# A fused attention and feed-forward kernel on one core: wider stores of the last block, a merged projection burst, a new sequence

## The chip, the cores and the metric

The kernel runs on one core of one Trainium2 chip. The metric is the device time of one execution in microseconds (us), as the median of several runs. The engines are TensorE (PE; its weight loads are PEld), VectorE (DVE), ScalarE (ACT), GpSimd (POOL) and SyncE (SP), which computes nothing and only issues DMAs. ACT and POOL issue DMAs too.

## The reference

Eight batches of eight heads go through linear attention with 128 random features; the result, 4608 rows of 512, goes through a two-layer feed-forward network with a hard-swish.

```python
def phi(x):                              # x: q or k, scaled; omega: (128, 64)
    proj = np.einsum('bhsd,md->bhsm', x, omega)
    h = proj - np.sum(x * x, axis=-1, keepdims=True) / 2.0
    return np.exp(h - np.max(h, axis=-1, keepdims=True)) / np.sqrt(m)
kv = np.einsum('bhsm,bhsd->bhmd', k_p, v); z = np.sum(k_p, axis=2)
num = np.einsum('bhsm,bhmd->bhsd', q_p, kv)
attn = num / (np.einsum('bhsm,bhm->bhs', q_p, z)[..., None] + 1e-06)
x = attn.transpose(0, 2, 1, 3).reshape(4608, 512)
h = x @ w_in                             # (512, 2048)
out = (h * np.clip(h + 3.0, 0.0, 6.0) / 6.0) @ w_out   # (2048, 512), float32
```

## The kernel before

**Tiling.** A batch has 576 rows: 512 "main" rows and 64 leftover rows. Attention runs batch by batch (`attention(b)`, b from 0 to 7). The feed-forward part runs over nine blocks of 512 rows: block b is the main rows of batch b, and block 8 is the 64 leftover rows of all eight batches, gathered in the tile `xS`. So partition p of block 8's output is row 512 + (p mod 64) of an even batch (p below 64) or of the odd batch after it (p from 64), and the four groups of 128 rows, r = 0 to 3, are the four pairs of batches. In the output tensor the two halves of a group lie 576 x 512 elements apart.

**Projections.** For b of 3 and more the products of k and q with omega are issued in bursts (`burst`, lines 749 to 798; matmuls at lines 766 and 769). A burst covers a few column groups ("doubles" of 128 rows) of k and q. A burst of two doubles takes two PSUM banks, one of four doubles takes four; the ring has eight banks in all. `BURSTS` gives five bursts per batch: one of two doubles (the leftover rows) and four of four doubles (main rows). ACT reads each bank with an exponential (kp at line 785, qpT at line 794), and DVE takes a row maximum.

**Feed-forward.** The first layer is `mm1` (line 1047); in blocks 7 and 8 it is a seven-product form of a 2 x 2 block product (`mm1_pair`, line 1126). The second layer is `products(blk)` (line 1305), called P0 to P6 here, again a seven-product form. DVE adds the pieces (line 1321): u3 after P3, C22 after P4, u4, and C21 after P5; ACT copies C11 (line 522). For block 8 the seventh product is cut into three pieces by `last_product` (matmuls at line 1371, additions C12 at line 1379): piece 0 is 256 columns wide, pieces 1 and 2 are 128 wide. Sums of activations that these products need are called S1 to S4 (line 1233), on POOL, some of block 8's on DVE.

**Stores of block 8.** `store` (DMA at line 1400) writes the three quarters C22, C21 and C11, each as two DMAs of 64 partitions by two row groups by 256 columns (128 KB). `last_product` (DMA at line 1383) writes each of its three pieces as two DMAs of 64 partitions (64 KB, and 32 KB for the narrow pieces). So there are twelve DMAs, on SP or ACT. Their destination patterns start with 64 rows, for instance `x[a, MAIN:S, 2 * i:2 * i + 2, c0:c1]` with the half `a` fixed: rows, then row groups, then columns. Blocks 0 to 7 are written by DMAs of 128 partitions from SP.

**What sets the order.** Every operation gets a number in the order in which the code creates it. `ORDER` lists, by these numbers, which operations each engine runs and in which sequence; an operation that two engines may run stands in the list of the one that does. Waits follow from the data. A list is strictly in order: what stands behind a waiting operation waits too. With the costs in the code the planner only orders the merged program; the numbers in `ORDER` fix the sequence on each engine. At the end the program waits for all stores.

Of the kernel before, what the change touches and what calls it, by code (L numbers as in the profile page):

```python
# [20 lines left out]
        118, 13, 124, 139, 144, 156, 115, 150, 168, 147, 153, 133, 127, 121, 142, 162, 165, 183, 171, 159, 175, 177,  # L21
        136, 185, 212, 130, 173, 197, 214, 179, 219, 254, 199, 187, 181, 242, 227, 189, 204, 202, 257, 229, 244, 217,
        222, 403, 404, 232, 234, 415, 247, 416, 417, 409, 410, 249, 411, 405, 406, 412, 418, 207, 421, 424, 252, 237,
        260, 280, 427, 430, 433, 300, 436, 288, 284, 282, 439, 286, 442, 306, 303, 445, 290, 315, 324, 309, 448, 451,
        312, 292, 294, 454, 296, 318, 457, 298, 333, 321, 583, 584, 331, 573, 337, 574, 335, 575, 339, 585, 586, 587,
        327, 341, 588, 576, 353, 345, 589, 343, 577, 329, 355, 366, 578, 579, 593, 368, 379, 371, 594, 595, 358, 392,
        590, 384, 381, 394, 397, 580, 374, 596, 597, 598, 361, 387, 603, 400, 599, 600, 621, 627, 624, 639, 636, 604,
        630, 642, 645, 505, 651, 492, 660, 501, 654, 495, 657, 486, 605, 507, 511, 606, 503, 607, 474, 509, 666, 483,
        498, 477, 480, 672, 608, 669, 513, 489, 609, 792, 610, 675, 519, 782, 515, 517, 527, 783, 539, 798, 541, 544,
        532, 551, 785, 529, 786, 563, 793, 556, 565, 568, 553, 695, 795, 796, 702, 799, 801, 802, 723, 805, 806, 709,  # L30
        736, 809, 815, 716, 824, 812, 818, 830, 741, 827, 839, 833, 842, 748, 854, 848, 845, 750, 860, 738, 760, 857,
        772, 753, 863, 765, 970, 774, 777, 971, 762, 980, 973, 974, 981, 883, 986, 983, 984, 890, 987, 989, 990, 897,
        1003, 1000, 1012, 997, 993, 994, 1006, 911, 1015, 924, 1021, 1027, 929, 1018, 936, 1033, 1030, 904, 926, 1048,
        1042, 1036, 941, 938, 1045, 960, 1051, 1174, 1158, 1159, 965, 948, 962, 1168, 953, 950, 1161, 1071, 1169,
        1162, 1078, 1171, 1172, 1175, 1085, 1177, 1178, 1191, 1092, 1185, 1188, 1194, 1200, 1215, 1203, 1112, 1206,
        1209, 1218, 1181, 1182, 1124, 1117, 1224, 1221, 1230, 1236, 1114, 1099, 1239, 1233, 1126, 1136, 1346, 1347,
        1129, 1141, 1138, 1356, 1148, 1349, 1150, 1153, 1350, 1357, 1259, 1287, 1359, 1360, 1266, 1362, 1365, 1366,
        1273, 1363, 1379, 1376, 1373, 1382, 1388, 1300, 1394, 1369, 1302, 1312, 1391, 1305, 1314, 1397, 1370, 1317,
        1406, 1336, 1409, 1418, 1338, 1403, 1421, 1412, 1280, 1424, 1427, 1550, 1341, 1534, 1535, 1544, 1454, 1537,
        1545, 1447, 1324, 1538, 1326, 1329, 1547, 1548, 1461, 1551, 1553, 1468, 1557, 1554, 1488, 1475, 1490, 1558,  # L40
        1500, 1493, 1561, 1502, 1505, 1512, 1579, 1517, 1514, 1567, 1582, 1524, 1570, 1526, 1600, 1529, 1591, 1564,
        1615, 1609, 1594, 1576, 1606, 1585, 1612, 1660, 1673, 1597, 1663, 1629, 1665, 1676, 1702, 1630, 1668, 1678,
        1689, 1632, 1633, 1692, 1639, 1694, 1705, 1681, 1718, 1707, 1640, 1697, 1731, 1721, 1642, 1723, 1643, 1734,
        1710, 1747, 1736, 1648, 1649, 1760, 1726, 1750, 1739, 1807, 1645, 1763, 1752, 1646, 1765, 1820, 1755, 1810,
        1652, 1812, 1653, 1836, 1768, 1823, 1776, 1825, 1815, 1777, 1839, 1849, 1828, 1841, 1779, 1852, 1865, 1844,
        1854, 1780, 1878, 1868, 1786, 1857, 1870, 1881, 1787, 1894, 1883, 1792, 1907, 1873, 1886, 1897, 1789, 1899,
        1793, 1790, 1910, 1902, 1939, 1912, 1795, 1796, 1915, 1799, 1800, 1923, 1924, 1933, 1934, 1926, 1927, 1936,
        1937, 1940, 1943, 1944, 1960, 1952, 1956,
    ],
    "SP": [  # L50
        0, 21, 17, 32, 23, 22, 31, 19, 25, 26, 27, 24, 29, 28, 30, 269, 270, 271, 469, 473, 472, 471, 470, 592, 602,
        468, 688, 467, 582, 693, 402, 692, 691, 694, 612, 689, 547, 535, 690, 559, 571, 572, 880, 879, 881, 804, 876,
        756, 744, 808, 768, 780, 882, 877, 781, 878, 992, 1067, 996, 1069, 1068, 1070, 932, 1065, 944, 968, 956, 969,
        1066, 1064, 1255, 1184, 1257, 1256, 1258, 1180, 1120, 1252, 1253, 1144, 1132, 1156, 1157, 1254, 1440, 1443,
        1445, 1446, 1368, 1372, 1444, 1441, 1320, 1442, 1344, 1308, 1332, 1345, 1496, 1520, 1508, 1532, 1556, 1560,
        1533, 1651, 1655, 1798, 1802, 1950, 1948, 1949, 1947, 1962, 1959,
    ],
    "ACT": [
        18, 20, 138, 119, 140, 145, 141, 157, 148, 154, 169, 151, 134, 166, 143, 211, 163, 184, 135, 172, 160, 196,
        176, 178, 241, 174, 186, 213, 225, 226, 180, 243, 182, 203, 190, 218, 188, 233, 407, 413, 419, 422, 425, 281,  # L60
        238, 261, 431, 253, 434, 428, 301, 289, 285, 437, 440, 287, 307, 443, 304, 446, 310, 449, 316, 452, 313, 455,
        325, 319, 297, 299, 295, 352, 334, 322, 336, 340, 332, 458, 342, 328, 338, 354, 378, 377, 330, 367, 344, 380,
        346, 393, 375, 362, 388, 401, 622, 591, 628, 625, 640, 631, 581, 601, 637, 643, 652, 646, 493, 661, 506, 655,
        496, 658, 502, 508, 512, 487, 504, 475, 478, 481, 673, 484, 499, 490, 667, 510, 526, 514, 611, 676, 538, 670,
        516, 520, 528, 518, 540, 550, 784, 561, 562, 787, 564, 696, 698, 700, 708, 705, 707, 703, 731, 726, 729, 701,
        724, 735, 728, 715, 714, 710, 737, 712, 816, 717, 810, 719, 813, 721, 819, 746, 828, 759, 831, 825, 840, 843,
        834, 770, 846, 722, 849, 761, 771, 855, 773, 861, 864, 858, 972, 888, 886, 884, 891, 893, 889, 896, 895, 900,
        975, 1004, 1001, 902, 898, 903, 920, 923, 998, 1013, 1007, 914, 912, 916, 1016, 1022, 1019, 1028, 917, 1034,
        1031, 907, 905, 910, 909, 1043, 1037, 946, 1049, 1052, 947, 1046, 1160, 949, 1076, 1072, 1074, 1163, 1084,
        1083, 1081, 1079, 1077, 1086, 1090, 1088, 1091, 1093, 1192, 1095, 1111, 1186, 1098, 1189, 1201, 1204, 1195,  # L70
        1134, 1123, 1207, 1216, 1210, 1125, 1097, 1225, 1219, 1222, 1231, 1237, 1102, 1100, 1105, 1137, 1234, 1240,
        1104, 1348, 1149, 1351, 1264, 1262, 1265, 1293, 1288, 1292, 1267, 1271, 1260, 1290, 1272, 1269, 1274, 1276,
        1296, 1299, 1380, 1295, 1279, 1374, 1311, 1377, 1383, 1278, 1389, 1395, 1313, 1392, 1334, 1335, 1398, 1407,
        1337, 1410, 1419, 1404, 1422, 1413, 1281, 1283, 1285, 1425, 1286, 1428, 1536, 1459, 1457, 1455, 1460, 1450,
        1448, 1539, 1453, 1452, 1484, 1464, 1462, 1467, 1466, 1487, 1469, 1471, 1473, 1489, 1499, 1476, 1478, 1501,
        1480, 1481, 1474, 1513, 1562, 1523, 1568, 1525, 1580, 1571, 1592, 1565, 1583, 1601, 1595, 1577, 1607, 1586,
        1613, 1661, 1662, 1674, 1598, 1664, 1675, 1610, 1677, 1616, 1631, 1669, 1690, 1671, 1691, 1703, 1693, 1682,
        1706, 1684, 1719, 1698, 1720, 1711, 1700, 1722, 1732, 1733, 1735, 1713, 1727, 1748, 1749, 1740, 1762, 1729,
        1742, 1751, 1764, 1809, 1756, 1758, 1811, 1769, 1822, 1816, 1771, 1824, 1837, 1818, 1840, 1850, 1831, 1829,
        1853, 1845, 1866, 1847, 1867, 1858, 1879, 1869, 1880, 1860, 1882, 1874, 1895, 1887, 1889, 1898, 1876, 1909,  # L80
        1903, 1911, 1905, 1916, 1918, 1928, 1946, 1951, 1955, 1963, 1954, 1958,
    ],
    "DVE": [
        16, 10, 11, 5, 4, 12, 123, 15, 7, 14, 125, 8, 116, 146, 9, 126, 191, 158, 128, 122, 155, 6, 209, 170, 167,
        152, 149, 239, 194, 129, 161, 164, 224, 131, 137, 198, 220, 200, 255, 201, 215, 221, 228, 216, 256, 230, 245,
# [317 lines left out]
def _emit(nc, es, q, k, v, omega, w_in, w_out, out):  # L403
    B, H, S, D = q.shape
# [11 lines left out]
    MAIN = 512  # L416
    TU = [(0, 2), (2, 6), (6, 10), (10, 14), (14, 18)]
    HALVES = [(0, 2), (2, 4)]
    SPLIT = 3
    ROWS = 3  # L420
    BURSTS = [[(0, 2)], [(2, 6)], [(6, 10)], [(10, 14)], [(14, 18)]]
    RP = 2.0
    FAST = 4
    APACE = 0.06
# [80 lines left out]
    op = G.op  # L505
# [987 lines left out]
```

The softmax here doesn't subtract the row's maximum and nothing guards it: scores larger than these inputs give would overflow.

## Time and profile before

| what | value |
|---|---|
| median of 3 runs | 308.26 us (307.58 to 308.68) |
| the profiled execution | 308.06 us |
| its span in the trace | 306.2 us |
| granted TensorE clock, mean | 0.998 |
| PE busy | 297.7 us (97%) |
| DVE busy | 245.7 us (80%) |
| POOL busy | 233.7 us (76%) |
| ACT busy | 212.8 us (69%) |
| median DMA of 128 KB, output from SP, issue to landing | 2.5 us |
| last matmul starts / ends | 301.17 / 301.39 us |

The time of an execution is about 1.9 us longer than the span that the trace covers. A busy PE is a modelled quantity: matmuls overlap. Times below are counted from the start of the span. The DMA rows give packets, megabytes and the time that the packets took as a share of sixteen DMA engines over the window that was asked for, so that share x 16 x window is the engine time used.

### The profile page before, as it was taken

The page shows a single profiled execution, that of the slowest core. Times are in us where ns is not written, and L with a number is a line of the kernel's source. Part 1 is how long each engine was busy: PE and PEld are TensorE (multiplying, and loading weights), DVE is VectorE, ACT ScalarE, POOL GpSimd, SP SyncE. Part 2 cuts the span into 40 slices and gives each one's busy share as a digit, 9 for nine tenths or more (in the row PEclk, how much of TensorE's full clock was granted, in tenths as well). Part 3 has the DMA queues.
Part 4 walks back from the last instruction along what each step waited for, and adds up shares of the span by engine and source line. Part 5 has one row for each costly group of instructions (what it writes and reads, how often), then busy time and mean ns, then how long its engine had stood idle before and what let it go on. Part 6 is the DMA issues. An engine that isn't in the chain of part 4 may idle for free.

```text
span 306.2 us, 7368 instructions
## 1 busy us (share of the span) xinstructions
PE 297.7 (97%) x2798; PEld 210.4 (69%) x2798; DVE 245.7 (80%) x539; ACT 212.8 (69%) x511; POOL 233.7 (76%) x247
## 2 busy tenths in 40 slices
PE   7999999999999999999999999999999999999993
PEld 5668866545785468646856586647764788888883
DVE  3978887779898885798596877896889898999953
ACT  4995997578959972889477758876875876675300
POOL 2775657089894989799989896988845999999950
PEclk9999999999999999999999999999999999999999
DMA  8999999999972999999949984998906000210125
GB/s 224 297 187 187 269 163 153 209 206 181 194 187 35 165 143 182 242 155 208 175 104 124 217 222 112 131 130 215 207 20 190 9 0 3 94 45 3 69 88 120
DMA packets 90147, 44.88 MB, mean 147 GB/s; under 512 B 57984, under 2 KB 87808, under 8 KB 90112
## 3 DMA queue, kind: packets, MB, share of 16 engines
q1 hardware_dynamic: 62368, 30.98, 43.5%
q0 software_dynamic: 26592, 12.46, 34.1%
q10 hardware_dynamic: 1152, 0.98, 1.2%
q8 instruction: 22, 0.36, 0.5%
q14 instruction: 13, 0.11, 0.2%
HBM read 36.73 MB, written 9.44 MB: 151 GB/s over the span
## 4 chain that ended last, share of the span: by engine, by line
PE 79%; POOL 10%; DMA 4%; DVE 2%; issue 1%; SPq 1%; ACT 1%; POOLq 0%
PE p L1305 28%; PE p L1047 25%; PE p L1126 5%; PE p L1217 4%; POOL gT L1233 3%; PE p L1192 3%; PE p L978 3%; DMA wi<-in_moe_w_in_dram 3%; POOL s L1233 3%; PE p L950 2%; PE p L766 2%; PE p L769 2%; DMA q<-in_q_dram 1%; SPq L621 1%; PE p L830 1%
## 5 line engine op out<-in xcount | busy, mean ns | idle before, releaser
L1047 PE MATMUL p<-xT,wi 128*128 128x512 f16 x384 | 90.3, 379 | 0.0
L1055 DVE SCALAR_TENSOR_TENSOR gT<-tsb,p 128x512 f16<-128x512 f16 x96 | 62.8, 679 | 12.4 <-ACT tsb L1053 11.6
L1053 ACT ACTIVATE tsb<-p 128x512 f16<-128x512 f32 x96 | 55.4, 600 | 16.5 <-PE p L1047 12.3
L1047 PEld LDWEIGHTS p<-xT,wi 128*128 128x128 f16 x384 | 35.4, 98 | 38.0 <-issue 1.1
L1305 PE MATMUL p<-wo,gT 128*128 128x256 f16 x368 | 45.8, 273 | 0.1
L1233 POOL TENSOR_TENSOR s<-gT 128x512 f16<-128x512 f16 x30 | 34.8, 1161 | 6.8 <-DVE gT L1055 4.8
L1233 POOL TENSOR_TENSOR gT<-gT,s 128x512 f16<-128x512 f16 x31 | 35.8, 1155 | 5.2 <-PE p L1305 3.0
L1233 POOL TENSOR_TENSOR s<-gT,s 128x512 f16<-128x512 f16 x31 | 35.8, 1156 | 4.9 <-DVE gT L1055 2.9
L1305 PEld LDWEIGHTS p<-wo,gT 128*128 128x128 f16 x368 | 35.0, 98 | 6.1 <-issue 0.8
L1233 POOL TENSOR_TENSOR gT<-gT 128x512 f16<-128x512 f16 x31 | 36.1, 1164 | 2.4
L934 POOL TENSOR_TENSOR vc<-v,cc 128x512 bf16<-128x512 f32 x24 | 25.4, 1057 | 12.3 <-DVE cc L928 7.4
L790 DVE TENSOR_REDUCE mx<-kp 128x4 f32<-128x512 bf16 (+1 forms) x50 | 29.9, 619 | 5.0 <-ACT kp L785 5.0
L794 ACT ACTIVATE qpT<-p 128x512 bf16<-128x512 f32 (+1 forms) x50 | 26.9, 564 | 8.6 <-PE p L769 8.6
L785 ACT ACTIVATE kp<-p 128x512 bf16<-128x512 f32 (+1 forms) x50 | 26.2, 559 | 9.3 <-PE p L769 8.6
L1305 PE MATMUL p<-t,gT 128*128 128x256 f16 x256 | 31.4, 273 | 0.0
L994 DVE TENSOR_TENSOR xb<-p,rec 128x256 f16<-128x256 f32 (+1 forms) x64 | 28.8, 471 | 0.6
L621 POOL DMA_DIRECT2D qb<-in_q_dram x28 | 19.5, 705 | 11.5 <-PE p L1047 9.6
L1305 PEld LDWEIGHTS p<-t,gT 128*128 128x128 f16 x256 | 24.3, 98 | 5.1 <-issue 1.2
L522 ACT COPY p<-p 128x256 f32<-128x256 f32 (+1 forms) x46 | 17.7, 398 | 13.2 <-PE p L1126 5.6
L1174 ACT ACTIVATE tsb<-p 128x512 f16<-128x512 f32 x32 | 18.8, 598 | 6.5 <-PE p L1126 3.9
L621 POOL DMA_DIRECT2D kb<-in_k_dram x21 | 16.5, 786 | 7.1 <-PE p L1047 7.1
L1176 DVE SCALAR_TENSOR_TENSOR gT<-tsb,p 128x512 f16<-128x512 f16 x32 | 21.0, 679 | 0.9 <-ACT tsb L1174 0.8
(132 smaller groups left out, 580.4 us busy)
## 6 DMA issues: line engine op xcount, KB each, us to landing
v<-in_v_dram SPq DMA_DIRECT2D x14, 512.0 KB, 4.9
out_dram<-osb SPq DMA_DIRECT2D x14, 512.0 KB, 3.3
kb<-in_k_dram POOLq DMA_DIRECT2D x14, 256.0 KB, 5.4
qb<-in_q_dram POOLq DMA_DIRECT2D x14, 256.0 KB, 5.6
wo<-in_moe_w_out_dram POOLq DMA_DIRECT2D x8, 256.0 KB, 8.2
wi<-in_moe_w_in_dram POOLq DMA_DIRECT2D x3, 512.0 KB, 7.4
q<-in_q_dram SPq DMA_DIRECT2D x4, 256.0 KB, 4.5
vl<-in_v_dram SPq DMA_DIRECT2D x8, 128.0 KB, 4.1
```

Source lines behind the costliest of these rows:

```text
L621: lambda E: E.dma_start(dst, src), prio + 0.001 * turn_of[0], reads=gate, writes=keys,
L785: op("ACT", actt(128 * (d1 - d0)), lambda E, lh=lh, ko=ko, part=part: E.activation(ko, out_of(part, 0, lh)[0].rearrange("p (x m) -> p x m" ...
L790: op("DVE", dvet(128 * (d1 - d0)), lambda E, ko=ko, mo=mo: E.reduce_max(mo, ko, axis=AX.X), p0 + 0.01, reads=[("kp", 0, d, lh) for d in ra ...
L794: op("ACT", actt(128 * (d1 - d0)), lambda E, lh=lh, part=part: E.activation(qd[:, part[0]:part[1], lh, :], out_of(part, 1, lh)[0].rearrang ...
L934: return E.tensor_tensor(vcm[:, :, 0:D], v32[:, m, :, :], cbc, ALU.mult)
L994: op("DVE", dvet(128 * n), lambda E: E.tensor_tensor(xv(i0, i1), psum()[:, :, :, 0:64], rbc, ALU.mult), t + 0.01, reads=[vn, ("rec", ru)], ...
L1047: ins = E.matmul(ring.t[vh.slot], wi[:, c, 128 * f:128 * f + 128], xv[:, c, :], start=(c == 0), stop=(c == NJ - 1))
L1053: op("ACT", actt(512), lambda E: E.activation(tsb[tu][:], ring.t[vh.slot], AF.Relu, bias=0.5, scale=1.0 / 6.0), t - 0.1, reads=[vh], write ...
L1055: op("DVE", dvet(512), lambda E: E.scalar_tensor_tensor(gT[gu][:, f, :], tsb[tu][:], 1.0, ring.t[vh.slot], ALU.min, ALU.mult), t - 0.1, re ...
L1176: op("DVE", dvet(512), lambda E, v=v, tu=tu, dst=dst: E.scalar_tensor_tensor(dst(), pieces(tsb[tu][:]), 1.0, pieces(v.ring.t[v.slot]), ALU ...
L1233: op(engines, {"POOL": 0.07 + n / 455.0, "DVE": 0.1 + n / 850.0}, lambda E: E.tensor_tensor(dst, x, y, ALU.subtract if minus else ALU.add) ...
L1305: ins = E.matmul(ring.t[v.slot][:, 256 * j:256 * j + 256], a[:, f, 128 * j:128 * j + 128], w[:, f, :], start=(first and f == 0 and j == 0) ...
```

## The change

Three things change.

1. The last block's stores take 128 partitions each. Each quarter is now two DMAs, one for each row group r, of 128 partitions by 256 columns (128 KB), and each piece of the last product is one DMA. That makes nine. The destination pattern now starts with the two halves `a`, then the 64 rows, then the columns.
2. `BURSTS` merges the leftover doubles with the first four main doubles into one burst that takes six PSUM banks. There are four bursts per batch instead of five, for b = 3 to 7.
3. All five lists of `ORDER` are new. The five burst operations and three stores that are gone shift the numbers: the main sequence of operations is otherwise the same, so a number below 702 means the same operation as before, and from there on it is one to five lower (up to eight lower at the very end).

With the numbers counted out, PE's list ends P3, P3, P4, then pieces 2 and 1 of the last product, P5, P5, piece 0. It used to end P3, P3, P4, P5, P5, pieces 2, 0, 1. On SP the last block's stores are now C22 (r = 2), C11 (r = 1), C11 (r = 0), piece 1, C21 (r = 2); on ACT C22 (r = 3), piece 2, C21 (r = 3), piece 0. Before, SP began with one half of C11. On DVE, S4 number 3 of block 8 now stands before u3; it stood between u3 and C22. S4 number 2 moves from POOL to DVE, also before u3.

```diff
 ORDER = {
     "PE": [
...
-        1937, 1940, 1943, 1944, 1960, 1952, 1956,
...
+        1790, 1791, 1910, 1897, 1928, 1918, 1919, 1794, 1795, 1929, 1921, 1922, 1931, 1932, 1935, 1953, 1950, 1938,
+        1939, 1947,
     "SP": [
...
-        1533, 1651, 1655, 1798, 1802, 1950, 1948, 1949, 1947, 1962, 1959,
...
+        1555, 1650, 1646, 1793, 1797, 1941, 1946, 1945, 1952, 1943,
     "ACT": [
...
-        1903, 1911, 1905, 1916, 1918, 1928, 1946, 1951, 1955, 1963, 1954, 1958,
...
+        1942, 1955, 1944, 1949,
...
-    BURSTS = [[(0, 2)], [(2, 6)], [(6, 10)], [(10, 14)], [(14, 18)]]
+    BURSTS = [[(0, 2), (2, 6)], [(6, 10)], [(10, 14)], [(14, 18)]]
...
-            for x in range(2):
-                op(("SP", "ACT"), {"SP": 0.9 * w / 1024, "ACT": 0.9 * w / 1024}, lambda E, x=x, j=j, e0=e0, e1=e1: E.dma_start(
-                    ends[x, MAIN:S, j, 256 + e0:256 + e1], osb[64 * x:64 * x + 64, j, 256 + e0:256 + e1]),
-                   t, reads=[("osb", j, 1, n)], writes=[("out", 8, j, e0, x)], group="doutl%d_%d" % (n, x), inc=16, lat=1.1,
-                   name="outl%d" % n, issue=0.65, packet=84.0)
+            op(("SP", "ACT"), {"SP": 1.8 * w / 1024, "ACT": 1.8 * w / 1024}, lambda E, j=j, e0=e0, e1=e1: E.dma_start(
+                ends[:, MAIN:S, j, 256 + e0:256 + e1], osb[:, j, 256 + e0:256 + e1]),
+               t, reads=[("osb", j, 1, n)], writes=[("out", 8, j, e0)], group="doutl%d" % n, inc=16, lat=1.1,
+               name="outl%d" % n, issue=0.65, packet=84.0)
...
         if blk < 8:
-            parts = [(0, 128, out[blk * S:blk * S + MAIN, :].rearrange("(p r) e -> p r e", r=4)[:, 2 * i:2 * i + 2, c0:c1])]
+            parts = [(2 * i, 2, out[blk * S:blk * S + MAIN, :].rearrange("(p r) e -> p r e", r=4)[:, 2 * i:2 * i + 2, c0:c1])]
         else:
             x = out.rearrange("(t a s) e -> a s t e", a=2, s=S)
-            parts = [(64 * a, 64, x[a, MAIN:S, 2 * i:2 * i + 2, c0:c1]) for a in range(2)]
+            parts = [(r, 1, x[:, MAIN:S, r, c0:c1]) for r in (2 * i, 2 * i + 1)]
...
+            src = osb[:, r:r + n, c0:c1] if n > 1 else osb[:, r, c0:c1]
```

## The prediction

> **What bounds the kernel now.** I read the page first, then the chain of waits over the last 20 us, then the timeline of PE and the DMA view of the last block's stores.
>
> ```profile
> span 306.2 us, 7368 instructions
> ...
> PE 297.7 (97%) x2798; PEld 210.4 (69%) x2798; DVE 245.7 (80%) x539; ACT 212.8 (69%) x511; POOL 233.7 (76%) x247
> ...
> PE 79%; POOL 10%; DMA 4%; DVE 2%; issue 1%; SPq 1%; ACT 1%; POOLq 0%
> ```
>
> PE is busy for 297.7 of 306.2 us. Of the other 8.5 us, 4.8 lie behind the last matmul (306.2 - 301.4), where the last stores are issued and land. By the table of busy time by stretches, 2.04 us lie in the first 10 us, 1.05 in the next 20, and so only some 0.6 in the rest. A new sequence has little idle time to win; the tail has 4.8 us.
>
> ```profile
> 299.63 1.33 PE p L1371 x16
> ...
> 300.99 0.42 DVE osb L1379
> ...
> 301.43 0.29 DVE osb L1379
> ```
>
> This is the end of the chain: the last product (L1371), then DVE's additions. After it only DMAs run. The timeline:
>
> ```profile
> 298.20 0.68 DVE L1321 TENSOR_TENSOR osb<-p,u 128x512 f32<-128x512 f32 x1
> ...
> 301.44 2.60 ACTq L1383 DMA_DIRECT2D out_dram<-osb  x4
> 302.35 1.24 SPq L1383 DMA_DIRECT2D out_dram<-osb  x2
> ```
>
> The first row is C22. The other two show that the issues queue: six stores of the last product, about 0.65 us each, keep ACT issuing until 304.04.
>
> **Part 1, the stores: how many DMA engines work.** The DMA view from 295.5 to 305.1 us holds just the last block's twelve stores.
>
> ```profile
> DMA packets 1344, 1.05 MB, mean 109 GB/s; under 512 B 192, under 2 KB 1344, under 8 KB 1344
> ...
> q1 hardware_dynamic: 736, 0.59, 29.1%
> q10 hardware_dynamic: 608, 0.46, 21.6%
> ```
>
> 192 tiny packets for twelve stores are 16 each: I read that as one closing packet from each of 16 engines. The two shares are 50.7% of 16 engines over 9.6 us: 77.9 us of engine time for the block's 1024 KB. Spread over 16 engines that is 4.9 us, well hidden under the issues.
>
> All twelve stores have a destination that begins with 64 rows, and every other transfer here begins with 64 or 128: each divides into 16 equal shares along its first dimension. The new destinations begin with a dimension of **two** (the halves of a pair, far apart in memory), then the 64 rows. No row shows how such a transfer is shared out. The bounds are 16 engines, as in every row, and two engines, if the sharing goes along the first dimension, as all rows would allow. I take two: rows and halves can't be joined into one dimension of 128, since they are not evenly spaced, and the code names no other cut.
>
> The Trainium skill, page "DMA: Bandwidth & Descriptors", section "Why a DMA increments its semaphore by 16 and not by 1", speaks against this change: the number of engines is the largest up to 16 that divides the slowest dimension of both sides. By it the new stores run on two engines, 64 packets of 1 KB each, where the old ones ran on 16; no row here shows a transfer below 16. The same page's section "Rules for kernel authors" speaks for the change: transfers to disjoint partition halves are no gain, and one of 128 partitions is to be used. By that rule alone the sum would be the sixteen-engine case below.
>
> Next the price of a packet on one engine, with three rows. Loads with packets of 1 KB, from 188.4 to 189.2 us:
>
> ```profile
> q1 hardware_dynamic: 295, 0.30, 105.7%
> ```
>
> 105.7% x 16 x 0.8 us / 295 = 45.9 ns for 1 KB. Stores with packets of 4 KB, from 264 to 264.6 us:
>
> ```profile
> q1 hardware_dynamic: 61, 0.25, 102.4%
> ```
>
> That is 102.4% x 16 x 0.6 / 61 = 161 ns for 4 KB, or 40.3 ns for 1 KB. The old half-width stores above took 77.9 us / 1024 = 76 ns for 1 KB. So one engine needs 40 to 76 ns for each KB. I take 45.9: same packet size, and, like the new stores, 128 partitions; the 64-partition stores read only half of the partitions with all engines, which may be why they are slow.
>
> With two engines, 1024 KB x 45.9 ns / 2 = **23.5 us** in which both work without a pause, against 4.9. The ends are 1024 x 40.3 / 2 = 20.6 us and 77.9 / 2 = 39.0 us. From a cover of 2.6 us of issues it has become the longest thing in the tail: what is late next is the DMA engines themselves.
>
> When do they start? SP's list now opens with C22, where it opened with half of C11 (issued at 295.82). SP waits for C22, and the two C11 stores queue behind it; nobody but the end waits for them. C22 needs P4, whose second half is 8 matmuls from 296.76: 8 x 0.109 us ends at 297.63. DVE started u3 0.2 us after PE's product, so C22 starts at 297.83 (S4 number 3, 0.71 us, no longer stands between u3 and C22) and ends at 298.5. S4 numbers 2 and 3 now lie ahead of u3: 2 x 0.71 us in a DVE wait of 2.80 us for PE, so they cost nothing; if that cover went, they would push C22 by 1.4 us. Issue at 298.5. The store issued at 295.82 had its first packets near 297.1, 1.35 us later. So packets run from 299.85. All nine are issued by about 302.5, before the first four (512 KB, 11.8 us) are through, so the engines don't starve.
>
> Packets end at 299.85 + 23.5 = 323.35. Before, the last packet was at 305.0 and the span ended at 306.2, so 1.2 us follow: a span of 324.55.
>
> **Part 2, the merged burst.** PE's timeline shows what a burst displaces.
>
> ```profile
> 87.38 0.28 PE L766 MATMUL p<-om,kT 64*128 64x128 bf16 x4
> ...
> 87.70 1.92 PE L1305 MATMUL p<-wo,s 128*128 128x256 f16 x16
> 89.56 0.40 PE L766 MATMUL p<-om,kT 64*128 64x128 bf16 x8
> ...
> 90.10 0.61 PE L1305 MATMUL p<-t,gT 128*128 128x256 f16 x4
> ```
>
> From a burst's first matmul to the next product's it is 0.32 us for two doubles and 0.54 for four, 0.11 a double. Six doubles would take 0.76 instead of 0.86: 0.10 saved, five times, **0.5 us**. What it may cost: the burst waits until six of the eight banks are free, and the product behind it on PE waits too. The old pair asked for two and four. If each of the five waited for two banks more, at 0.56 us of ACT each (mean of the 50 instructions of L785), that is 5.6 us. I take no wait: in the new list the burst stands right behind the second half of a product, or among mm1, where one or two banks are held, and ACT, 69% busy, has had 2.6 us or more of products since the burst before. Ends: 0.5 gained to 5.1 lost.
>
> **Part 3, the new lists.** The body has about 3.7 us of PE idle time (2.04 + 1.05 + 0.6), the most that can be gained. A poorer order may lose as much. No single row decides; I take zero. At the end, P5 now runs behind two pieces of the last product; the last matmul stays at 301.4, since the same matmuls remain.
>
> **Sum.** 324.55 - 0.5 = 324.05 of span. The profiled execution was 308.06 for a span of 306.2, so 1.86 us lie around it: **325.9 us**. The median of the runs, 308.26, is 0.2 above the profiled one, which changes nothing here.
>
> **The rivals.**
>
> *Two engines at the old price.* If 76 ns for 1 KB is what a scattered 1 KB write costs one engine whoever reads beside it, the data takes 39.0 us: 325.9 + 15.5 = 341.4. For it: it is the only row of 1 KB stores. Against it: the loads at 45.9 ns.
>
> *Sixteen engines* (the other side: faster). If transfers are shared out over 16 engines whatever their first dimension, 1024 KB take 4.9 us or less and hide under the issues. Then the end is piece 0: the last matmul ends at 301.39, C12 takes 0.43 us, ACT issues at 301.9, where the last of the old six issues started at 303.5. Span 306.2 - 1.6 - 0.5 = 304.1, time 306.0. It decides only close to sixteen engines: with eight, 77.9 / 8 = 9.7 us of packets from 299.85 on end at 309.6, behind the 305.0 of before. For it: all 16 closing packets in each row. Against it: none of those rows has a first dimension under 64.
>
> *Sixteen engines, but the six-bank bursts wait.* Then 306.0 + 0.5 + up to 5.1: some 309 to 311. Against it: the old sequence loses under 0.6 us in the body after 30 us, though it asks for four banks at once 20 times.
>
> **How the numbers follow.** Two engines near the load price: 0.65. Two engines at the old store price: 0.17. Sixteen engines: 0.13. Sixteen with waiting bursts: 0.05. The predicted time is the first, 325.9. Its low end is 20.6 in place of 23.5 us and 3 us more gained in the lists: 325.9 - 2.9 - 3 = 320. The high end is the second case with 1.6 us lost: 343. That range leaves out the sixteen-engine cases, 0.18. A measurement of this kernel can tell about 0.3% (0.9 us) from no change. Faster by more: 0.13. Within: 0.02. Slower by more: 0.65 + 0.17 + the waiting-burst case, less its share within, 0.85 in all.
>
> **What would show it.** In the view of the last block's DMAs: a stretch of over 20 us in which a mean of about two of sixteen DMA engines is busy (12%), some 45 GB/s, and closing packets fewer than 16 a store. Stores would land 3 us or more after their issue, and the last ones over 15 us. The last matmul should still end near 301 us. 16 closing packets a store and landings of 2.5 us would refute it. If the packets take 76 ns, only the price was wrong; if PE's end moved by over 1 us, parts 2 or 3 were misjudged.

## The result, and the profile after

The changed kernel takes 326.36 us (median of four runs, 325.86 to 327.37), the kernel before 308.47 us in the same comparison. The ratio is 1.057, with a 95% interval of 1.050 to 1.064: slower by 17.9 us. The profiled execution took 326.54 us for a span of 324.3 us.

The page of the changed kernel, with the tenths of PE and of the DMA engines in 40 slices:

```profile
span 324.3 us, 7371 instructions
...
PE 295.8 (91%) x2792; PEld 212.2 (65%) x2796; DVE 247.1 (76%) x541; ACT 208.4 (64%) x501; POOL 234.7 (72%) x251
...
PE   8999999999999999999999999999999999999000
...
DMA  7999999998979978998699797990340003011111
...
PE 72%; POOL 7%; DMA 6%; ACT 3%; DVE 2%; issue 1%; SPq 1%; POOLq 0%; ACTq 0%
```

PE is busy about as long as before, but its row ends in three empty slices: 24 us in which no matmul runs. The DMA row shows what runs there, at a tenth of the sixteen engines. The chain's PE share falls from 79% to 72%, mostly because the span grew behind it. The chain over the end:

```profile
299.55 0.89 PE p L1371 x8
...
300.46 0.42 DVE osb L1379
```

The compute work is through at 300.88 us; it was at 301.72. The last matmul ends at 300.42, 0.97 us earlier than before. So the loss is all behind it: 23.9 us against 4.8. The DMA view of that time, from 299 to 324 us:

```profile
DMA  0110111111111111111111111111111111111100
GB/s 13 33 33 21 26 15 49 59 34 49 49 46 49 49 45 48 46 46 48 46 47 49 49 48 48 47 48 46 47 47 46 48 46 49 49 49 46 49 31 0
DMA packets 1171, 1.06 MB, mean 42 GB/s; under 512 B 18, under 2 KB 1170, under 8 KB 1170
...
q1 hardware_dynamic: 650, 0.59, 7.5%
q10 hardware_dynamic: 520, 0.46, 5.4%
```

18 tiny packets for nine stores are two a store, where twelve stores had 192. The shares are 12.9% of sixteen engines, a mean of 2.06. The data packets run from 299.24 to 323.42 us: 24.2 us for 1024 KB. The GB/s row shows that they begin slowly: 13 to 33 GB/s in the first six slices, 3.75 us, and mostly 45 to 49 after that. The granted clock is 0.54 from 302 us on (0.968 over the span); no matmul runs there, so this cannot be what makes the time. The timeline of the last instructions:

```profile
297.25 0.69 DVE L1321 TENSOR_TENSOR osb<-p,u 128x512 f32<-128x512 f32 x1
...
300.31 4.96 ACTq L1399 DMA_DIRECT2D out_dram<-osb  x1
...
302.07 5.36 SPq L1382 DMA_DIRECT2D out_dram<-osb  x1
...
305.31 4.23 ACTq L1382 DMA_DIRECT2D out_dram<-osb  x1
307.48 3.15 SPq L1399 DMA_DIRECT2D out_dram<-osb  x1
```

The first row is C22; its stores are issued at 297.97. The four others are the last issues, which took 3.2 to 5.4 us each where one took about 0.65: the last is done at 310.62. In SP's waits from 240 us on, the final wait for the stores is the row

```profile
SPq L1464 <- DMA out_dram<-osb: 12.9, 3, 4.8
```

### The profile page after: what moved, and what is told of

Same layout as the page of the kernel before. It is cut to its first block, busy times and chain, and to the rows that moved or that the text cites. A ratio compares the mean times of both kernels' runs of the same rounds, so it can differ in the third digit from the quotient of the medians.

```text
span 324.3 us, 7371 instructions
## 1 busy us (share of the span) xinstructions
PE 295.8 (91%) x2792; PEld 212.2 (65%) x2796; DVE 247.1 (76%) x541; ACT 208.4 (64%) x501; POOL 234.7 (72%) x251
## 4 chain that ended last, share of the span: by engine, by line
PE 72%; POOL 7%; DMA 6%; ACT 3%; DVE 2%; issue 1%; SPq 1%; POOLq 0%; ACTq 0%
PE p L1305 29%; PE p L1047 21%; PE p L1126 6%; DMA wi<-in_moe_w_in_dram 5%; PE p L1217 4%; POOL s L1233 3%; PE p L766 2%; PE p L978 2%; PE p L950 2%; DMA q<-in_q_dram 2%; PE p L769 2%; POOL gT L1233 1%; PE p L1192 1%; PE p L830 1%; ACT tsb L1053 1%
## 5 line engine op out<-in xcount | busy, mean ns | idle before, releaser
L1047 PE MATMUL p<-xT,wi 128*128 128x512 f16 x384 | 89.1, 379 | 0.0
L1053 ACT ACTIVATE tsb<-p 128x512 f16<-128x512 f32 x96 | 55.2, 605 | 17.9 <-PE p L1047 13.6
L1305 PE MATMUL p<-wo,gT 128*128 128x256 f16 x368 | 45.9, 273 | 0.0
L1233 POOL TENSOR_TENSOR gT<-gT,s 128x512 f16<-128x512 f16 x30 | 34.7, 1157 | 6.5 <-PE p L1305 4.3
L1233 POOL TENSOR_TENSOR s<-gT 128x512 f16<-128x512 f16 x31 | 35.9, 1157 | 4.1 <-DVE gT L1055 2.1
L1233 POOL TENSOR_TENSOR gT<-gT 128x512 f16<-128x512 f16 x30 | 35.0, 1166 | 2.3
L934 POOL TENSOR_TENSOR vc<-v,cc 128x512 bf16<-128x512 f32 x25 | 26.5, 1061 | 7.5 <-DMA v<-in_v_dram 3.8
L994 DVE TENSOR_TENSOR xb<-p,rec 128x256 f16<-128x256 f32 (+1 forms) x64 | 28.1, 469 | 0.4
L1321 DVE TENSOR_TENSOR u<-p 128x512 f32<-128x512 f32 x16 | 11.0, 690 | 12.4 <-PE p L1305 12.3
```

The lines of the kernel that those rows point to most:

```text
L934: return E.tensor_tensor(vcm[:, :, 0:D], v32[:, m, :, :], cbc, ALU.mult)
L994: op("DVE", dvet(128 * n), lambda E: E.tensor_tensor(xv(i0, i1), psum()[:, :, :, 0:64], rbc, ALU.mult), t + 0.01, reads=[vn, ("rec", ru)], ...
L1047: ins = E.matmul(ring.t[vh.slot], wi[:, c, 128 * f:128 * f + 128], xv[:, c, :], start=(c == 0), stop=(c == NJ - 1))
L1053: op("ACT", actt(512), lambda E: E.activation(tsb[tu][:], ring.t[vh.slot], AF.Relu, bias=0.5, scale=1.0 / 6.0), t - 0.1, reads=[vh], write ...
L1233: op(engines, {"POOL": 0.07 + n / 455.0, "DVE": 0.1 + n / 850.0}, lambda E: E.tensor_tensor(dst, x, y, ALU.subtract if minus else ALU.add) ...
L1305: ins = E.matmul(ring.t[v.slot][:, 256 * j:256 * j + 256], a[:, f, 128 * j:128 * j + 128], w[:, f, :], start=(first and f == 0 and j == 0) ...
```

## The experiments

The theory was: the nine stores run on two DMA engines, because the largest number up to sixteen that divides the first dimension of their destination is two; that alone makes the loss, and the rest of the change is worth about nothing. The rivals: the lists or the merged burst make it; or stores of 128 partitions into scattered rows are slow for another reason. Runs with one number were taken once; medians stand with their number of runs.

### The stores alone, and the rest without them

**e2_new_stores_only**: the kernel before, with the nine stores.

```diff
 # before's lists and BURSTS; the last block's DMAs as in the change
-            parts = [(64 * a, 64, x[a, MAIN:S, 2 * i:2 * i + 2, c0:c1]) for a in range(2)]
+            parts = [(r, 1, x[:, MAIN:S, r, c0:c1]) for r in (2 * i, 2 * i + 1)]
```

> The kernel before with only its last block's stores changed to nine of 128 partitions; bursts and lists stay, C11's two stores go first. Theory: 2 closing packets a store, the first packet near 297.2 us and then 24.2 us of packets as in the changed kernel, so the last at 321.4, a span of 322.4 and a time near 324.3 us. Rival (the lists lose the time): 308 us.

324.23 us (4 runs), ratio to before 1.049 [1.044, 1.055]. The DMA view from 299 to 324 us:

```profile
DMA packets 1170, 1.05 MB, mean 42 GB/s; under 512 B 18, under 2 KB 1170, under 8 KB 1170
```

Two closing packets a store, and data packets from 299.76 to 323.12 us. In this execution the last matmul ended only at 304.05, 3.6 us later than in the changed kernel, and the span (324.0) is that of the changed kernel all the same: the end of PE has stopped to matter. The stores alone lose 15.2 us (324.23 against 309.02 for the kernel before in the same comparison), most of the 17.9. The 2.1 us by which this kernel is faster than the changed one were expected from the earlier start of C11's stores, but the one trace, of the slowest of the four runs, does not show them.

**e1_old_stores**: the changed kernel with the twelve old stores.

```diff
-            parts = [(r, 1, x[:, MAIN:S, r, c0:c1]) for r in (2 * i, 2 * i + 1)]
+            parts = [(64 * a, 64, x[a, MAIN:S, 2 * i:2 * i + 2, c0:c1]) for a in range(2)]
...
```

> The changed kernel with its merged burst and new lists, but with the twelve 64-partition stores of before. Theory (the stores use two DMA engines because their destination begins with a dimension of two): 16 closing packets a store again, landings near 2.5 us, the last matmul where the changed kernel has it (300.4 us), a span near 304.8 us and a time of 306 to 307 us, so some 1.5 to 2 us under before. Rival (the new lists or the six-bank bursts lose the time): a time near 326 us. Rival (nothing but the stores matters, the lists give nothing): 308.3 us.

310.12 us (12 runs), ratio 1.0024 [0.9999, 1.0049]. The loss is gone and there are 16 closing packets a store again, but it is some 3 us above what was expected. The last matmul ended at 300.38, so the missing time lies behind it. The timeline there:

```profile
299.18 5.03 ACTq L1381 DMA_DIRECT2D out_dram<-osb  x2
```

Two issues with 4.05 us between them: ACT waits, from 299.69 to 303.74, for a semaphore that the landing of C21's first half raises. The second issue is half of a piece of the last product and needs nothing from C21. Both DMAs carry the same name in the code's list of written things: `("out", 8, j, e0, x)` in the last product and `("out", blk, i, c0, p0)` in `store` are equal where x and p0 are both 0. The planner takes them for two writes to one place and orders them. The kernel before has this wait too, but there it costs about 0.1 us, since its list issues the two in another order. In the changed kernel the names differ.

**e5_old_stores_free**: the same with that name changed.

```diff
-   t, reads=[("osb", j, 1, n)], writes=[("out", 8, j, e0, x)], ...
+   t, reads=[("osb", j, 1, n)], writes=[("outl", 8, j, e0, x)], ...
```

> As e1, with one key renamed. In e1 the scheduling ACT spent 4.05 us (299.69 to 303.74) on a wait for semaphore 166, which is the landing of C21's first half: the code of before gives a piece of the last product and a half of C21 the same key for 'bytes written', so that the piece waits for the half, though they write other bytes. With the lists of the changed kernel that wait stands in ACT's way; here the key has a name of its own. Theory: ACT issues without a gap, the last issue begins near 302.0 us, the last landing is near 304.5 us, the span 305.0 us and the time 2.5 us under e1, 307.6 us. Rival (the wait is of the chip, a limit on stores in flight): as e1, 310.1 us.

306.85 us (12 runs), ratio 0.9932 [0.9904, 0.996]. The needless wait was the 3 us. Lists and merged burst together, with the old stores, are 0.7% **faster** than before; the prediction had them at 0.5 us.

### What sets the number of engines

**e8_62_rows** and **e11_57_rows**: e5 with shorter stores, which leave out the last two, or the last seven, rows of each 64: 62 = 2 x 31 and 57 = 3 x 19. The diff is that of e8.

```diff
-   parts = [(64 * a, 64, x[a, MAIN:S, 2 * i:2 * i + 2, c0:c1]) for a in range(2)]
+   parts = [(64 * a, 62, x[a, MAIN:S - 2, 2 * i:2 * i + 2, c0:c1]) for a in range(2)]
...
```

> As e5, but each of the twelve stores leaves out the last two rows of its 64 (so the output lacks them): 62 partitions, and a destination that begins with 62 rows, evenly spaced, in one piece as before. Theory (the engines are the largest number up to 16 that divides the first dimension: 62 = 2 x 31): 2 closing packets a store, 31/32 of the data over two engines, 23.4 us of packets from 299.2 us on, a span near 323.6 us and a time near 325.6 us. Rival (only the two far-apart halves, or the 128 partitions, confine a store to two engines): 16 or 15 engines, a time like e5's, near 307.5 us.

> As the run with 62 rows a store, but with 57 of the 64 rows (the last seven rows of each group of 64 are left out of the output). 57 is 3 x 19. If the number of DMA engines is the largest up to 16 that divides the first dimension, three engines work: 3 closing packets a store; 912 KB at the 47.3 ns for 1 KB that two engines took in the changed kernel (24.2 us x 2 / 1024), divided by three, are 14.4 us from 299.1 us on, a span of 314.4 and a time of 316.6 us. If any destination that does not divide by 16 falls back to two engines: 21.6 us of packets, a time of 323.8 us. If the number of engines has to be a power of two, one engine works: 43 us of packets, 345 us.

325.38 us and 315.96 us, one run each. The DMA view of the run with 62 rows, from 298 to 323.2 us:

```profile
DMA packets 1141, 1.02 MB, mean 41 GB/s; under 512 B 24, under 2 KB 1140, under 8 KB 1140
...
q1 hardware_dynamic: 696, 0.63, 7.9%
q10 hardware_dynamic: 444, 0.38, 4.5%
```

and of the run with 57 rows, from 299 to 314 us:

```profile
DMA packets 1028, 0.91 MB, mean 60 GB/s; under 512 B 36, under 2 KB 1027, under 8 KB 1027
...
q1 hardware_dynamic: 613, 0.55, 11.3%
q10 hardware_dynamic: 414, 0.35, 7.1%
```

For twelve stores, 24 closing packets are two each and 36 are three each; the shares are 12.4% x 16 = 2.0 and 18.4% x 16 = 2.9 engines. Nothing else differs from e5, which takes 18.5 us less than e8: two rows fewer a store bring the loss back, seven fewer take half of it away. This shuts out a fall-back to two engines and a rule of powers of two.

The runs also price a packet. Two engines took 23.7 us for 992 KB with 64-partition sources: 23.7 x 2 / 992 = 47.8 ns a KB. With 128 partitions in the changed kernel it is 24.2 x 2 / 1024 = 47.3 ns. Three engines took 15.0 us for 912 KB: 49.3 ns. So the 76 ns of the old stores are no price of a 64-partition store; they arise when sixteen engines serve such stores at once.

**e3_rows_first**: 128 partitions and a destination that begins with 32 rows. Block 8's rows are put in another order, so that partition p holds row p div 4 of batch p mod 4; TensorE reads `xS` in that order, with neighbours 64 elements apart.

```diff
-   parts = [(r, 1, x[:, MAIN:S, r, c0:c1]) for r in (2 * i, 2 * i + 1)]
+   parts = [(r, 1, x[i, MAIN + 32 * (r % 2):MAIN + 32 * (r % 2) + 32, :, c0:c1]) for r in (2 * i, 2 * i + 1)]
...
+   xi = xS.rearrange("p j (k q s) -> p j k s q", k=2, q=4)
...
```

> The changed kernel, but the tokens of the last block are laid out so that partition p holds row p div 4 of batch p mod 4: the nine stores still have 128 partitions and 128, 64 and 64 KB, and 1 KB or 512 B packets to rows that lie as far apart, but their destination begins with 32 rows and then four batches. Theory (first dimension): 16 closing packets a store, landings near 2.5 us, a time near 305.5 us, the best of all. Rival (a store of 128 partitions with packets of 1 KB to scattered rows, or its issue, is slow in itself): near 326 us as in the changed kernel. What may spoil the size: the strided reads of the last block's tokens by TensorE, VectorE and GpSimd, which no row shows; 0 to 3 us.

322.78 us (6 runs), ratio 1.0445 [1.0398, 1.0492], where 305.5 was expected: a miss, for another reason. The stores do what the theory says (16 closing packets each, median landings of 2.2 to 2.5 us, the span ends 3.4 us behind the last matmul), but the last matmul ends at 315.33. The groups by line show why; first the kernel before, then this one (busy time and mean ns of one stand behind the bar):

```profile
L1126 PE MATMUL p<-xS,wi 128*128 128x256 f16 x32 | 5.8, 273 | 0.0
```

```profile
L1133 PE MATMUL p<-xS,wi 128*128 128x256 f16 x32 | 16.1, 604 | 0.0
```

The same matmul takes 604 ns in place of 273 when its moving operand has steps of 64 elements. Over the 48 matmuls that read `xS` that is 0.33 x 48 = 16 us, about what the last matmul is late.

**e7_rows_first_copy**: the same stores, with the reordering done by four ACT copies of 128 x 512 so that TensorE reads contiguous data.

```diff
+   op("ACT", actt(512), lambda E, j=j: E.copy(
+       xT[0][:, j, :].rearrange("p (k s q) -> p k s q", k=2, q=4),
+       xS[:, j, :].rearrange("p (k q s) -> p k s q", k=2, q=4)), ...
```

> As e3, but the tokens of the last block are put in their new order by four copies on ACT (0.6 us each, behind the last relu of block 6) into a tile that is free by then, so that TensorE, VectorE and GpSimd read them in one piece. In e3 the strided reads took TensorE 1.03 us for two matmuls of 256 columns that take 0.38, and its end came 14.9 us later. Theory: TensorE ends near 300.4 us, the nine stores of 128 partitions use 16 engines, the span is near 304.0 us and the time near 306 us. Rival (a store of 128 partitions is slow beside the others for another reason that e3's late end hid): over 310 us.

308.61 us (12 runs), ratio 0.9966 [0.9941, 0.9991]: 18 us below the changed kernel, but above e5. ACT's timeline and PE's waits from 236 to 246 us:

```profile
239.29 4.02 ACT L1098 COPY xT<-xS 128x512 f16<-128x512 f16 x4
```

```profile
PE p L1308 <- ACT p L521: 2.5, 1, 2.5
```

The copies took 1.0 us each where 0.6 was reckoned with, and PE waited 2.5 us for the copy queued behind them. The last matmul ended at 304.22, 3.8 us later than in the changed kernel; what makes the rest is not shown. Nine stores of 128 partitions on sixteen engines are cheap all the same: 3.4 us from the last matmul to the end of the span, where e5's twelve half stores take 4.2.

### The lists and the merged burst

**e4_split_bursts**, **e6_split_bursts_free** and **e10_split_again**: e1 and e5 with the leftover burst separate again, its two parts back to back in PE's list.

```diff
-    BURSTS = [[(0, 2), (2, 6)], [(6, 10)], [(10, 14)], [(14, 18)]]
+    BURSTS = [[(0, 2)], [(2, 6)], [(6, 10)], [(10, 14)], [(14, 18)]]
...
```

> The kernel of e1, but each merged burst is again a burst of two doubles with a burst of four right behind it, in the place of the merged one. Theory (a burst has a cost of its own of about 0.1 us): the last matmul ends 0.3 to 0.5 us later than in e1, and the time is as much longer. Rival (six banks at once make TensorE wait, so splitting helps): the last matmul ends earlier than in e1, by up to 2 us.

> As e4, with the same key renamed: bursts split again, all else as in e5. What e1 and e4 showed (310.1 against 309.1 us) speaks against the prediction's half microsecond gained by merging. Theory (six banks at once make TensorE wait): 0.3 to 1 us under e5. Rival (the difference of e1 and e4 was chance): within 0.3 us of e5. The prediction's own step: 0.3 to 0.5 us over e5.

> The kernel with the new lists, the separate leftover bursts and the twelve old stores once more, on the same chip as the run above, so that the two can be set side by side: 306.4 us, last matmul at 299.5, 4.2 us behind it.

e4: 309.11 us (12 runs), ratio 0.9994 [0.9966, 1.0023], against 310.12 for e1. e6: 306.45 us (6 runs), ratio 0.9901 [0.987, 0.9932], against 306.85 for e5. e10, on another chip: 306.42 us (6 runs), ratio 0.9914 [0.988, 0.9948]. Separate bursts are faster by 1.0 and 0.4 us by the medians; the intervals of each pair overlap a little, the sign is the same. The single runs of e1 (309.30 to 310.66) and e4 (308.68 to 309.79) lie mostly apart, those of e5 (306.29 to 309.50) and e6 (305.88 to 307.27) do not, so the 0.4 us alone would show nothing. PE's waits of e5, and then of e6, have one row that differs:

```profile
PE p L764 <- DVE osb L1319: 0.8, 1, 0.8
```

```profile
PE p L765 <- DVE osb L1320: 0.5, 1, 0.5
```

The last batch's first burst waits at 220 us for the banks that DVE's additions still hold; six banks come free 0.3 us later than four. Where the rest of the 0.4 to 1.0 us goes is not shown. One profile more or less doesn't settle it either: the last matmul of the same kernel ended at 299.54 in e6 and at 300.22 in e10.

### The best of both

**e9_rows_spread**: separate bursts and nine stores on sixteen engines; the reordering is done by eight copies of 128 x 256, one a batch, seven of them where POOL was idle.

```diff
+   op("ACT" if b == 7 else "POOL", 0.5, lambda E: (E.copy if b == 7 else E.tensor_copy)(
+       xI[:, :, 256 * (b // 4):256 * (b // 4) + 256].rearrange("p j (s q) -> p j s q", q=4)[:, :, :, b % 4],
+       xS[:, :, 64 * b:64 * b + 64]), ...
```

> The new lists with separate leftover bursts, and nine stores of 128 partitions whose destinations begin with 32 rows, each followed by its four batches. The leftover rows are put in that order by eight copies of 128 x 256 elements, one for each batch, into a tile of their own: seven on POOL, where it stood idle for 4.8 us before 223.7 us, and one on ACT behind the last relu of block 6. Theory (sixteen engines serve a first dimension of 32, and such stores take less time behind the last matmul than twelve half stores): last matmul at 299.5 as in the kernel with old stores and separate bursts, then 3.4 us, a span of 302.9 and with 2.2 us around it 305.1 us, some 1.0 to 1.3 us under that kernel in the same call. Rival (the copies cost what the stores gain): POOL's seven copies take over 0.7 us each, or the one on ACT delays the next product's release, PE waits 1 us or more around 224 or 240 us, and the time is that of the old stores or above it, 306.3 to 308.

306.19 us (12 runs), ratio 0.9929 [0.9898, 0.996], beside e10's 306.42 on the same chip. Its DMA view from 299 to 303.5 us, and the copies:

```profile
DMA packets 1296, 1.05 MB, mean 233 GB/s; under 512 B 144, under 2 KB 1296, under 8 KB 1296
...
q1 hardware_dynamic: 720, 0.59, 40.3%
q10 hardware_dynamic: 576, 0.46, 31.4%
```

```profile
L890 POOL COPY xI<-xS x7: 751/757/761, 219.2 to 224.1; 128x256 f16<-128x256 f16 x7
```

144 closing packets are 16 a store. 71.7% x 16 x 4.5 us = 51.6 us of engine time for 1024 KB, 50 ns a KB: two thirds of the 76 ns of the half stores before. The tail is 3.35 us behind a last matmul at 300.25; e10 has 4.2 us behind one at 300.22. These 0.8 us in the two profiles are not found again in the medians, 0.2 us apart with ranges of 305.14 to 308.94 and 305.75 to 307.32. Each copy took 0.75 us, and PE lost 0.3 us waiting for POOL near 224 us. So the full intent of the change, wide stores on all engines, can be had, and is worth no more than can be told from nothing; the 0.7 to 1.0% by which e5, e6, e9 and e10 beat the kernel before comes with the new lists and a shorter tail, and which of the lists' moves gives it was not tested.

## Why the prediction was right, point by point

| term | predicted | measured | difference |
|---|---|---|---|
| first data packet, us | 299.85 | 299.24 | -0.6 |
| 1024 KB on two engines, us | 23.5 | 24.2 | +0.7 |
| last packet to end of span, us | 1.2 | 0.9 | -0.3 |
| merged burst, us | -0.5 | in the first row | +0.5 |
| around the span, us | 1.86 | 2.24 | +0.4 |
| time of the profiled execution, us | 325.9 | 326.54 | +0.6 |

The time is 0.6 us off, but the terms are off by -0.9 and +1.6 us together: part of the agreement is luck, as the errors cancel.

**Two engines: right.** Two closing packets a store, 2.06 engines at work, and two and three engines on demand in e8 and e11. The Trainium skill, page "DMA: Bandwidth & Descriptors", section "Why a DMA increments its semaphore by 16 and not by 1", gives the rule that all these runs follow: the largest number up to 16 that divides the slowest dimension of both sides. The runs show it for first dimensions of 2, 57, 62, 32 and 64 of the destination; in none was the source's the smaller. The same page's section "Rules for kernel authors" advises one transfer of 128 partitions in place of two halves. With the change's destination that lost 17.9 us; with e9's the tail is 0.8 us shorter in the profiles and the medians show no gain.

**The price: right, 3% low.** 45.9 ns from the 1-KB loads against 47.3. The 47.3 is a mean, and the prediction saw neither of its parts: two engines at about 47 GB/s need 2 x 1024 B / 47 = some 44 ns a KB, less than was taken, and the slow first 3.75 us make up for it. Why the stores begin slowly is not shown. The choice between ends far apart was decided by the reason given for it: e8 shows 47.8 ns for half-width stores when only two engines serve them, so the 76 ns belonged to sixteen engines at once.

**The start: 0.6 us early.** It was reckoned with lists worth zero. C22 started at 297.25 and not at 297.83 because PE was ahead: its last matmul ended 0.97 us earlier. "The lists 0" is the term that was mis-sized: e5, e6 and e10 are 2 to 3 us faster than before with the old stores, some 0.6 us of which is a shorter tail (4.2 us against 4.8). Behind a transfer of 24 us little of that can be seen. The prediction also has six stores that keep ACT issuing until 304.04; its own rows show four on ACT and two on SP. Nothing rests on it.

**The merged burst: wrong in sign, by e1 and e4.** The prediction took "no wait" and gained 0.5 us from fewer starts of bursts. PE does wait, 0.3 us more at one place, and e1 and e5 are 1.0 and 0.4 us slower than their counterparts with separate bursts. It lies within the ends that were named (0.5 gained to 5.1 lost).

**"All nine are issued by about 302.5": wrong, without effect.** The last issue was done at 310.62. The prediction counted an issue at its usual length; in the kernels whose stores ran on two engines the later issues took several us each, and why is not shown. It cost little if anything, since the DMA row stays near the share of two engines; had an issuing engine been needed for something else, it could have cost up to 5.4 us each time.

**The rivals.** Two engines at the old price, 341.4, is shut out by the 47.3 ns. Sixteen engines were priced at 306.0; e9, which is that case with separate bursts and copies, measured 306.19. Part of that agreement is the lists, which that case counted at zero; the condition was false.

## What to carry to other kernels

Before a DMA's pattern is reshaped, work out how many engines will serve it from its first dimension (on both sides, though these runs vary mainly the destination's), and count the closing packets in the profile: two where sixteen were expected means one eighth of the engines, here a mean of 42 GB/s against 233 in e9. A pattern with a small outer dimension can often be had with another order of the rows, but the reordering has its own price on the engine that does it, and a matmul must not pay it. Where an edit makes a wait go, look whether it went with the work or with a name: two things that share a name in a dependency list wait for each other.

## What the runs showed of the hardware that was not expected

- An issue on ACT's or SP's queue took 3.2 to 5.4 us instead of 0.65 once the queues held several stores for two engines (also 2.0 to 4.6 us in the run with 62 rows). In no run with sixteen engines did an issue of the last block take over 0.8 us.
- A matmul whose moving operand steps by 64 elements took 604 ns instead of 273 (e3). The Trainium skill, page "SBUF — State Buffer", section "Specifications (TRN2)", tells of lines of 16 bytes and a penalty where each access goes to a new one; these steps of 128 bytes agree with that, though no run here shows that the lines are the cause.
- Stores of 64 partitions cost 76 ns a KB of one engine's time with sixteen engines at work in the kernel before and 61 in e10 (75.6% x 16 x 5.2 us / 1024 KB, from 299 to 304.2 us), but 47.8 ns with two; why 76 in one and 61 in the other is not shown. Stores of 128 partitions cost 47 to 50 ns with either.
